# Packing normed attention outputs into dense rows for the output projection, and moving weight loads to SyncE

## The chip, the cores and the metric

The kernel runs on one core of a Trainium2 chip. The metric is the device time of one execution in microseconds. Before the change it is 2338.6 us, the median of three runs (2338.2 to 2338.93). The profiled execution spans 2337.2 us.

A core has five engines with an instruction stream each. TensorE (PE) multiplies matrices; its loads of the stationary operand are listed as PEld. VectorE (DVE) and ScalarE (ACT) work element by element, GpSimd (POOL) does the same and issues transfers, and SyncE (SP) only issues transfers. Each engine takes its instructions in order, and waits on semaphores for what others produce.

## The reference

Four attention layers on x of shape 1 x 2048 x 640, with 32 heads of 20 columns. Layers 0 and 2 (kind A) look back over a window of 256 positions; layers 1 and 3 (kind B) are full, with no mask.

```python
def ref(x, wqkv, wo, windowed):
    q, k, v = split(x @ wqkv)                      # 32 heads of 20 columns
    scores = einsum("bhqd,bhkd->bhqk", q, k) * 20 ** -0.5
    if windowed:
        scores = where((i - j >= 0) & (i - j < 256), scores, -1e9)
    p = softmax(scores)
    o = einsum("bhqk,bhkd->bhqd", p, v)
    return o.transpose(0, 2, 1, 3).reshape(B, S, D) @ wo

x = A_x                                            # A_x: 1 x 2048 x 640, bf16
x = x + ref(layernorm(x), A_wqkv, A_wo, True)
x = x + ref(layernorm(x), B_wqkv, B_wo, False)
x = x + ref(layernorm(x), A_wqkv, A_wo, True)
x = x + ref(layernorm(x), B_wqkv, B_wo, False)
```

## The kernel before

The positions are cut into 4 chunks of 512 (NC = 4, C = 512) and the heads into 8 groups of 4 (G = 8). A unit is one chunk of queries with one head group. Its scores, three banks of 512 columns at a time, go from TensorE to PSUM; ScalarE takes the exponential of all three banks with one instruction; TensorE multiplies the result with the values. One such round is a tick. Everything else is written as generators that a small scheduler at build time interleaves between the scores and the values of a tick: normalisation, the q, k and v projections, the tails of units, the output projections. Each gives up its turn with `yield`: `("wait", n)` sleeps n ticks, `("hold", cost)` keeps an accumulation together, `("pe", cost)` charges TensorE time. Layer l + 1 starts on a chunk before layer l has finished the others, so a windowed unit stands between full ones.

In a head group, head j of the group has the 20 rows from 32j, and its 12 other rows carry nothing for the output. The output weights are loaded in the same form, 8 tiles of 128 rows of which 80 count:

```python
    def load_wop(w):
        v = wo_in[w].rearrange("(g j e) f -> j e g f", g=G, j=4)
        for j in range(4):
            nc.sync.dma_start(out=wop[32 * j : 32 * j + DH, :, :], in_=v[j])
```

The tail of a unit divides by the sums of the softmax and leaves the normed output of head group g in `on[:, g, :]`:

```python
    def t_tail(l, c, g, on, oT):
        # ... row sums, reciprocal, transpose, spread over rows into PSUM bank zb, with waits of 2 ticks ...
        nc.vector.tensor_tensor(out=on[:, g, :], in0=oT[:], in1=zb, op=ALU.mult)     # L1043
        drop_m(mb)
        yield ("pe", 0.3)
        fill(3)
        ready.add(("tail", l, c, g))
        if (l, c, g) == (3, NC - 1, G - 3):
            push("before_last", t_before_last(), 0, 8.0)
        if g == G - 1:
            # ... push t_out(l, c) and, below layer 3, the work of layer l + 1 on this chunk ...
```

The output projection of a chunk multiplies and adds the residual, in 8 accumulations of 8 matmuls. The very last chunk is split: `t_before_last` does head groups 0 to 5 early, `t_out` only the last two.

```python
    def t_out(l, c):
        # ...
        for qb in range(4):
            for i in range(2):
                mb = yield from take_m()
                yp = ps[:, mb, 0:HD]
                g0 = G - 2 if last else 0
                for g in range(g0, G):
                    nc.tensor.matmul(                                                # L532
                        yp, lhsT=on[:, g, qb * P : (qb + 1) * P],
                        rhs=wop[:, g, i * HD : (i + 1) * HD],
                        start=(g == g0), stop=(g == G - 1),
                    )
                    if g < G - 1:
                        yield ("hold", 0.14)
                # ... x_sb = x_sb + yp on VectorE (L541) ...
        # ...
        n = out_n[0] = out_n[0] + 1
        if n < len(out_seq) and out_seq[n] != out_seq[n - 1]:
            load_wop(out_seq[n])
```

The q and k projections take their weights in 160 KB blocks of 128 columns. A block is asked for some ticks ahead, and from then on the projection waits at least 4 ticks before it is built in:

```python
    def get_w(l, n, c, i):
        t = wqkp.tile([P, KD, P], BF16, name="wqk", tag="wqk")
        wtick[l, n, c, i] = state["tick"] + 4
        if l or c:
            a = n * D + i * P
            nc.gpsimd.dma_start(out=t[:], in_=wq_view[l % 2][:, :, a : a + P])       # L318
            return t
        # ... the first chunk of layer 0 is cut out of a larger load ...
```

The normalisation transposes each tile of 128 positions, and in layers 0 and 1 puts two matmuls ahead of it whose result nobody reads. They keep TensorE busy. The program also counts activity and adds such matmuls in `keep_clock` where the count is low:

```python
            mb = yield from take_m()                                                 # in t_ln
            for _ in range(2*(l<2)):
                unread(mb)
            # ... 5 transposes of 128 columns into ps[:, mb] ...

    def unread(b):
        nc.tensor.matmul(                                                            # L611
            ps[:, b, :], lhsT=ident[:], rhs=masks[:, 0, :], start=True, stop=True
        )
        state["heat"] += 1.0

                warmth = 1.76 if state["unit"] >= woven else 1.0                     # in the main loop
                state["least"] = warmth * n_b / 3 if state["unit"] < index[3, 1, 0, None] else 0.0
                load_ahead()
                r = rate(t)
                pump(r, r + 0.1)          # advance waiting tasks by r
                keep_clock()
```

SyncE issues all loads of queries, keys and values of the units (`load_unit`: nine for a full unit, eight for a windowed one), the output weights and the final stores. GpSimd issues the weight blocks and the stores of q, k and v to DRAM.

Of the kernel before, what the change touches and what calls it, by code (L numbers as in the profile page):

```python
# [12 lines left out]
ALU = mybir.AluOpType  # L13
ACT = mybir.ActivationFunctionType

P = 128
# [3 lines left out]
DH = 20  # L20
NT = S // P
KD = D // P
G = 8
C = 512
NC = S // C
EPS = 1e-5
SCALE = DH ** -0.5
HD = D // 2
# [21 lines left out]
def kernel(  # L50
# [10 lines left out]
    nc = tc.nc  # L61
# [27 lines left out]
    wo_in = (A_wo, B_wo)  # L89
# [5 lines left out]
    wop = big.tile([P, G, D], BF16, name="wop", tag="wop")  # L95
# [13 lines left out]
    op = ps[:, 7, :]  # L109
# [6 lines left out]
    wq_view = [w.rearrange("(c p) f -> p c f", p=P) for w in wqkv_in]  # L116
# [3 lines left out]
    for h in range(2):  # L120
        for n in range(2):
            a = n * D + h * HD
# [3 lines left out]
        nc.sync.dma_start(out=x_sb[:, 4 * c : 4 * c + 4, :], in_=xin[:, 4 * c : 4 * c + 4, :])  # L126
    nc.sync.dma_start(out=wv_sb[1][:], in_=wq_view[1][:, :, 2 * D : 3 * D])

    def load_wop(w):
        v = wo_in[w].rearrange("(g j e) f -> j e g f", g=G, j=4)  # L130
        for j in range(4):
            nc.sync.dma_start(out=wop[32 * j : 32 * j + DH, :, :], in_=v[j])
# [3 lines left out]
        out=ident[:], in_=ident[:], compare_op=ALU.not_equal, fill=1.0,  # L136
# [6 lines left out]
    for m, b, ge in (  # L143
# [4 lines left out]
        v = masks[:, m, b * P : (b + 1) * P]  # L148
        nc.gpsimd.affine_select(
            out=v, in_=v, compare_op=ALU.is_ge if ge else ALU.is_gt, fill=0.0,  # L150
# [161 lines left out]
    def get_w(l, n, c, i):  # L312

        t = wqkp.tile([P, KD, P], BF16, name="wqk", tag="wqk")
        wtick[l, n, c, i] = state["tick"] + 4
        if l or c:
            a = n * D + i * P
            nc.gpsimd.dma_start(out=t[:], in_=wq_view[l % 2][:, :, a : a + P])  # L318
            return t
        tv = t[:].rearrange("p c (j m) -> p c j m", j=4)  # L320
        nc.gpsimd.memset(tv[:, :, :, DH:32], 0.0)
        src = raw[:, :, n * D + 80 * i : n * D + 80 * (i + 1)]
        nc.vector.tensor_copy(
            out=tv[:, :, :, 0:DH], in_=src.rearrange("p c (j e) -> p c j e", j=4)
        )
        wtick[l, n, c, i] = 0
        return t
# [48 lines left out]
    def t_ln(l, c):  # L376
        while ("x", l, c) not in ready:
            yield ("wait", 1)
        yield from room("xnT", "ln")
        for n in (1, 0):  # L380
            order = worder[l, n]
            if order and not any(e in wtiles for e in order):
                wtiles[order[0]] = get_w(*order[0])
        users[l, c] = 9 if (l, c) == (0, 0) else (11, 12, 11, 11)[l]
        mv = mvs.pop((l, c))
        rstd = lnp.tile([P, 4], F32, name="rstd", tag="rstd")
        nc.gpsimd.tensor_scalar(  # L387
            out=rstd[:], in0=mv[:, :, 1], scalar1=EPS, scalar2=1.0, op0=ALU.add, op1=ALU.mult
        )
        nc.gpsimd.tensor_tensor(out=rstd[:], in0=rstd[:], in1=nhalf[:], op=ALU.pow)  # L390
        yield ("wait", 2)
        nmr = lnp.tile([P, 4], F32, name="nmr", tag="nmr")
        nc.vector.scalar_tensor_tensor(
            out=nmr[:], in0=mv[:, :, 0], scalar=-1.0, in1=rstd[:], op0=ALU.mult, op1=ALU.mult
        )
        xt = xtp.tile([P, KD, C], BF16, name="xnT", tag="xnT")
        for i in range(4):
            xn = xnp.tile([P, D], BF16, name="xn", tag="xn")
            nc.vector.tensor_scalar(
                out=xn[:], in0=x_sb[:, 4 * c + i, :],  # L400
                scalar1=rstd[:, i : i + 1], scalar2=nmr[:, i : i + 1],
                op0=ALU.mult, op1=ALU.add,
            )
            yield ("wait", 1)
            mb = yield from take_m()
            for _ in range(2*(l<2)):
                unread(mb)
            trp = ps[:, mb, :].bitcast(BF16)[:, 0 : KD * P].rearrange("p (c m) -> p c m", c=KD)
            for dc in range(KD):
                nc.tensor.transpose(  # L410
                    out=trp[:, dc, :], in_=xn[:, dc * P : (dc + 1) * P], identity=ident[:]
                )
            evac(xt[:, :, i * P : (i + 1) * P], trp)
            drop_m(mb)
            yield ("pe", 0.4)
        xnT[l, c] = xt
        live["ln"] -= 1
        ready.add(("xnT", l, c))
# [98 lines left out]
    out_seq = [0] * 4 + [1, 0] * 4 + [1] * 4  # L517
    out_n = [0]

    def t_out(l, c):  # L520
        on = ons[l, c]
        last = (l, c) == (3, NC - 1)
        while last and "before_last" not in ready:
            yield ("wait", 1)
        assert out_seq[out_n[0]] == l % 2
        for qb in range(4):
            for i in range(2):
                mb = yield from take_m()
                yp = ps[:, mb, 0:HD]
                g0 = G - 2 if last else 0  # L530
                for g in range(g0, G):
                    nc.tensor.matmul(  # L532
                        yp, lhsT=on[:, g, qb * P : (qb + 1) * P],
                        rhs=wop[:, g, i * HD : (i + 1) * HD],
                        start=(g == g0), stop=(g == G - 1),
                    )
                    if g < G - 1:
                        yield ("hold", 0.14)
                xv = x_sb[:, 4 * c + qb, i * HD : (i + 1) * HD]
                had = part_o["t"][:, 2 * qb + i, 0:HD] if last else xv  # L540
                nc.vector.tensor_tensor(out=xv, in0=had, in1=yp, op=ALU.add)  # L541
                drop_m(mb)
                yield ("pe", 0.14)
            if l < 3:
                stats(l + 1, c, qb)
            else:
                nc.sync.dma_start(out=xout[:, 4 * c + qb, :], in_=x_sb[:, 4 * c + qb, :])
        ons.pop((l, c))
        ready.add(("out", l, c))
        ready.add(("x", l + 1, c))  # L550
        n = out_n[0] = out_n[0] + 1
        if n < len(out_seq) and out_seq[n] != out_seq[n - 1]:
            load_wop(out_seq[n])

    def t_before_last():

        on = ons[3, NC - 1]
        for qb in range(4):
            for i in range(2):
                mb = yield from take_m()  # L560
                yp = ps[:, mb, 0:HD]
                for g in range(G - 2):
                    nc.tensor.matmul(
                        yp, lhsT=on[:, g, qb * P : (qb + 1) * P],
                        rhs=wop[:, g, i * HD : (i + 1) * HD],
                        start=(g == 0), stop=(g == G - 3),
                    )
                    if g < G - 3:
                        yield ("hold", 0.14)
                xv = x_sb[:, 4 * (NC - 1) + qb, i * HD : (i + 1) * HD]  # L570
                nc.vector.tensor_tensor(
                    out=part_o["t"][:, 2 * qb + i, 0:HD], in0=xv, in1=yp, op=ALU.add
                )
                drop_m(mb)
                yield ("pe", 0.14)
        ready.add("before_last")
# [32 lines left out]
# [6 lines that stand above are left out]
# [382 lines left out]
    def t_tail(l, c, g, on, oT):  # L997
        def fill(count):

            for n in range(count * ((l, c, g) == (3, NC - 1, G - 1))):  # L1000
                nc.tensor.matmul(
                    ps[:, 0, :], lhsT=ident[:], rhs=masks[:, 0, :], start=True, stop=True
                )
# [3 lines left out]
        mb = yield from take_m()  # L1007
        warm_bank(mb)
        zp = ps[:, mb, 0:16]
        for qb in range(4):  # L1010
            nc.tensor.matmul(
                zp[:, 4 * qb : 4 * qb + 4], lhsT=oT[:, qb * P : (qb + 1) * P],
                rhs=sel4[:], start=True, stop=True,
# [11 lines left out]
        mb = yield from take_m()  # L1025
# [9 lines left out]
        mb = yield from take_m()  # L1035
        warm_bank(mb)
        zb = ps[:, mb, :]
        for qb in range(4):
            nc.tensor.matmul(  # L1039
                zb[:, qb * P : (qb + 1) * P], lhsT=spread4[:, qb, :], rhs=rT[:],  # L1040
                start=True, stop=True,
            )
        nc.vector.tensor_tensor(out=on[:, g, :], in0=oT[:], in1=zb, op=ALU.mult)  # L1043
        drop_m(mb)
        yield ("pe", 0.3)
        fill(3)
        ready.add(("tail", l, c, g))
        if (l, c, g) == (3, NC - 1, G - 3):
            push("before_last", t_before_last(), 0, 8.0)
# [5 lines left out]
    def t_zeros():  # L1055

        z = ka_all[:, G : G + 4, :].rearrange("p a b -> p (a b)")
        yield ("wait", 4)
        for n in range(2):
            nc.gpsimd.dma_start(  # L1060
                out=wop[:, 4 * n : 4 * n + 3, :].rearrange("p g f -> p (g f)"), in_=z[:, 0 : 3 * D]
            )
            nc.gpsimd.dma_start(out=wop[:, 4 * n + 3, :], in_=z[:, 0:D])
            yield ("wait", 1)
        load_wop(0)
        for t in (*kts, *qts):
            nc.gpsimd.dma_start(out=t[:], in_=z[:, 0 : t.shape[1]])
            yield ("wait", 1)
        ready.add("kts")
# [67 lines left out]
    with tc.manual_schedule():  # L1137
# [14 lines left out]
        n = 0  # L1152
# [54 lines left out]
        t = -1  # L1207
        ended = None
        closed = -2
        while ended is None or t < ended + 8:  # L1210
# [3 lines left out]
            if t < len(tiles) or banks:  # L1214
# [54 lines left out]
                i = 0  # L1269
# [115 lines left out]
```

## Time and profile before

| Stretch, us | ScalarE busy | TensorE busy | TensorE clock |
|---|---|---|---|
| 0 to 350 | 288.1 of 350.0 | 315.2 | 0.99 |
| 350 to 700 | 327.7 of 350.0 | 302.7 | 0.96 |
| 700 to 1165 | 441.2 of 465.0 | 395.8 | 0.96 |
| 1165 to 1640 | 455.7 of 475.0 | 401.7 | 0.99 |
| 1640 to 2337 | 666.8 of 697.2 | 577.3 | 0.57 |

The last stretch is layer 3 alone, with no q, k or v projection left. The clock is the share of full speed that TensorE was granted. The difference between length and busy time of ScalarE is its idle time, 157.7 us over the whole span.

The chain of work that ended last, by engine:

```
ACT 40%; PE 27%; issue 17%; DVE 13%; DMA 1%; POOL 1%; ACTq 0%; SPq 0%; DVEq 0%; POOLq 0%; another core or an unknown queue 0%
```

Two of the groups of transfers (how many, KB each, median us from issue to landing where the profile has it):

```
wqk<-in_B_wqkv_dram POOLq DMA_DIRECT2D x80, 160.0 KB, 3.8
wqk<-in_A_wqkv_dram POOLq DMA_DIRECT2D x70, 160.0 KB, 3.3
```

In a line of a group, the name of the code line comes first, then engine and operation, what is written from what is read, shape and count; after the bar the busy time in us and the mean of one in ns; after the second bar how long the engine sat idle just before these instructions, and what ended most of that. Matmuls overlap, so the mean of one is its latency and not its spacing. In a timeline, the first two columns are start and length in us, and the bracket at the end is the idle time before and what ended it.

### The profile page before, as it was taken

The page shows a single profiled execution, that of the slowest core. Times are in us where ns is not written, and L with a number is a line of the kernel's source. Part 1 is how long each engine was busy: PE and PEld are TensorE (multiplying, and loading weights), DVE is VectorE, ACT ScalarE, POOL GpSimd, SP SyncE. Part 2 cuts the span into 40 slices and gives each one's busy share as a digit, 9 for nine tenths or more (in the row PEclk, how much of TensorE's full clock was granted, in tenths as well). Part 3 has the DMA queues.
Part 4 walks back from the last instruction along what each step waited for, and adds up shares of the span by engine and source line. Part 5 has one row for each costly group of instructions (what it writes and reads, how often), then busy time and mean ns, then how long its engine had stood idle before and what let it go on. Part 6 is the DMA issues. An engine that isn't in the chain of part 4 may idle for free.

```text
span 2337.2 us, 40427 instructions
## 1 busy us (share of the span) xinstructions
PE 1992.5 (85%) x15613; PEld 722.9 (31%) x15773; DVE 1464.3 (63%) x2724; ACT 2179.5 (93%) x1753; POOL 271.1 (12%) x445
## 2 busy tenths in 40 slices
PE   8899988888888888888888898888888888888887
PEld 3444333333223332323323333333322222222222
DVE  6677775426646666656667644452577777777772
ACT  7788989899999988999899999999999999999997
POOL 3332311200200112001120013001000000000000
PEclk9999999999989999999999999999855565556556
DMA  5232321321300223102231023112210010011100
GB/s 183 81 103 80 107 65 56 90 68 48 89 21 25 58 68 90 43 14 58 70 99 31 17 82 107 41 28 76 65 30 27 26 38 27 27 35 39 31 14 12
DMA packets 84881, 132.57 MB, mean 57 GB/s; under 512 B 19760, under 2 KB 60080, under 8 KB 84688
## 3 DMA queue, kind: packets, MB, share of 16 engines
q1 hardware_dynamic: 65472, 76.80, 11.9%
q0 software_dynamic: 19216, 53.17, 7.8%
q8 instruction: 124, 2.03, 0.4%
q14 instruction: 69, 0.57, 0.1%
HBM read 98.70 MB, written 27.79 MB: 54 GB/s over the span
## 4 chain that ended last, share of the span: by engine, by line
ACT 40%; PE 27%; issue 17%; DVE 13%; DMA 1%; POOL 1%; ACTq 0%; SPq 0%; DVEq 0%; POOLq 0%; another core or an unknown queue 0%
ACT pt L1275 39%; PE ps L1244 7%; PE ps L353 5%; PE ps L532 4%; PE ps L1308 4%; DVE pt L1344 3%; PE ps L446 2%; PE ps L611 2%; DVE on L1043 1%; DVE st L304 1%; DMA wqk<-in_B_wqkv_dram 1%; ACT ka L1275 1%; DVE oT L830 1%; DVE raw_o L878 1%; PE ps L410 1%
## 5 line engine op out<-in xcount | busy, mean ns | idle before, releaser
L1275 ACT ACTIVATE pt<-ps 128x1536 bf16<-128x1536 f32 (+2 forms) x1641 | 2100.9, 1492 | 115.2 <-PE ps L1244 104.6
L1244 PE MATMUL ps<-qt,kt 32*128 32x512 bf16 x4008 | 644.6, 457 | 197.1 <-ACT pt L1275 164.2
L1308 PE MATMUL ps<-pt,vt 128*21 128x512 bf16 x3860 | 469.2, 458 | 5.1 <-issue 2.2
L1244 PEld LDWEIGHTS <-kt 32*128 32x128 bf16 x4008 | 191.0, 93 | 615.1 <-issue 592.0
L1344 DVE TENSOR_TENSOR pt<-pt,masks 128x1024 bf16<-128x1024 bf16 (+5 forms) x403 | 239.0, 626 | 131.5 <-ACT pt L1275 131.0
L611 PE MATMUL ps<-masks,ident 128*128 128x512 bf16 x672 | 231.7, 393 | 27.0 <-DVE rT L1030 9.6
L353 PE MATMUL ps<-xnT,wqk 128*128 128x512 bf16 x767 | 211.4, 388 | 24.8 <-DMA wqk<-in_B_wqkv_dram 4.2
L1308 PEld LDWEIGHTS <-vt 128*21 128x21 bf16 x3960 | 100.0, 90 | 319.1 <-issue 309.7
L304 DVE CAST st<-ps 128x512 bf16<-128x512 f32 x127 | 87.8, 691 | 154.4 <-PE ps L353 150.8
L532 PE MATMUL ps<-wop,on 128*128 128x320 bf16 x976 | 165.5, 312 | 6.9 <-DVE x_sb L541 2.5
L1244 PE MATMUL ps<-qa,ka 32*128 32x384 bf16 (+2 forms) x1408 | 116.8, 275 | 33.9 <-ACT pt L1275 28.8
L878 DVE TENSOR_SCALAR xnT<-ps 128x512 int32<-128x512 f32 x88 | 60.8, 691 | 106.3 <-PE ps L871 105.9
L1043 DVE TENSOR_TENSOR on<-oT,ps 128x512 bf16<-128x512 bf16 x128 | 87.5, 683 | 59.5 <-PE ps L1039 59.2
L830 DVE CAST oT<-ps 128x512 bf16<-128x512 f32 x112 | 76.9, 686 | 70.8 <-PE ps L1308 45.4
L446 PE MATMUL ps<-wv,xnT 128*128 128x320 bf16 x640 | 111.9, 309 | 7.0 <-DVE va L304 1.6
L541 DVE TENSOR_TENSOR x_sb<-x_sb,ps 128x320 bf16<-128x320 bf16 x120 | 57.9, 482 | 95.1 <-PE ps L532 94.9
L532 PEld LDWEIGHTS <-on 128*128 128x128 bf16 x976 | 90.2, 101 | 71.4 <-issue 38.4
L353 PEld LDWEIGHTS <-wqk 128*128 128x128 bf16 x830 | 71.3, 98 | 114.0 <-issue 49.2
L387 POOL TENSOR_SCALAR rstd<-mv 128x4 f32<-128x4 f32 x15 | 4.0, 265 | 815.6 <-DVE mv L374 815.5
L611 PEld LDWEIGHTS <-ident 128*128 128x128 bf16 x768 | 56.4, 97 | 126.2 <-issue 123.0
L1308 PE MATMUL ps<-pt,va 128*21 128x384 bf16 (+2 forms) x1408 | 77.6, 281 | 4.9 <-DVE pt L1344 2.9
L1244 PEld LDWEIGHTS <-ka 32*128 32x128 bf16 x1408 | 44.4, 92 | 101.2 <-issue 92.7
(107 smaller groups left out, 1790.9 us busy)
## 6 DMA issues: line engine op xcount, KB each, us to landing
vt<-v_d SPq DMA_DIRECT2D x48, 336.0 KB
kt<-k_d SPq DMA_DIRECT2D x192, 80.0 KB
wqk<-in_B_wqkv_dram POOLq DMA_DIRECT2D x80, 160.0 KB, 3.8
wqk<-in_A_wqkv_dram POOLq DMA_DIRECT2D x70, 160.0 KB, 3.3
k_d<-st POOLq DMA_DIRECT2D x75, 128.0 KB, 2.1
q_d<-st POOLq DMA_DIRECT2D x75, 128.0 KB, 2.1
qt<-q_d SPq DMA_DIRECT2D x384, 20.0 KB
v_d<-vs POOLq DMA_DIRECT2D x16, 336.0 KB, 3.1
```

The lines of the kernel that those rows point to most:

```text
L304: nc.vector.tensor_copy(out=out_, in_=in_)
L353: nc.tensor.matmul(pq, lhsT=wt[:, dc, :], rhs=xt[:, dc, :], start=(dc == 0), stop=(dc == KD - 1),)
L446: nc.tensor.matmul(pv, lhsT=xt[:, dc, i * P : (i + 1) * P], rhs=wv_sb[l % 2][:, dc, h * HD : (h + 1) * HD], start=(dc == 0), stop=(dc == K ...
L532: nc.tensor.matmul(yp, lhsT=on[:, g, qb * P : (qb + 1) * P], rhs=wop[:, g, i * HD : (i + 1) * HD], start=(g == g0), stop=(g == G - 1),)
L611: nc.tensor.matmul(ps[:, b, :], lhsT=ident[:], rhs=masks[:, 0, :], start=True, stop=True)
L830: nc.vector.tensor_copy(out=oT[:], in_=op)
L878: V.tensor_scalar(out=xi.bitcast(I32)[:, i * C : (i + 1) * C], in0=side["psum"], scalar1=SCALE * LOG2E * E23, scalar2=127.0 * E23, op0=ALU ...
L1043: nc.vector.tensor_tensor(out=on[:, g, :], in0=oT[:], in1=zb, op=ALU.mult)
L1244: nc.tensor.matmul(sp[:, i, col * P : (col + qn) * P], lhsT=u.k(kc, j), rhs=u.q(j, q0, qn), start=True, stop=True,)
L1275: nc.scalar.activation(out=pt[:, i:k, b0 * P :], in_=sp[:, i:k, b0 * P :], func=ACT.Exp, scale=SCALE,)
L1308: nc.tensor.matmul(op[32 * j : 32 * j + VW, q0 * P : (q0 + qn) * P], lhsT=u.v(kc, j), rhs=pg[:, i, col * P : (col + qn) * P], start=(first ...
L1344: nc.vector.tensor_tensor(out=pt_[:, i:k, b0 * P :], in0=pt_[:, i:k, b0 * P :], in1=mv_, op=ALU.mult,)
```

## The change

From layer 1 on, the normed output of a head group goes to one of three spare slots of `on` (5 to 7), and two ticks later SyncE is given transfers from SBUF to SBUF that copy the 20 rows of each head to their place in 640 dense rows, five blocks of 128. The output weights are loaded in the same dense form. The projection then takes 5 matmuls in an accumulation instead of 8. The last two head groups of the last chunk keep the old form, so that no transfer stands at the very end; the first part of that chunk takes 4 matmuls instead of 6. Layer 0 keeps the old form.

Two further things change. Weight blocks are loaded by SyncE instead of GpSimd. And the two unread matmuls ahead of the transposes are gone.

```diff
+    def packed(l, c):
+        return l > 0
+
-    def load_wop(w):
+    def load_wop(w, dense):
+        if dense:
+            nc.sync.dma_start(out=wop[:, 0:KD, :], in_=wo_in[w].rearrange("(b p) f -> p b f", p=P))
+            if w and out_n[0] == 4:
+                ...                      # once: groups 6 and 7 in the old form, for the last chunk
+            return
@@ get_w
-            nc.gpsimd.dma_start(out=t[:], in_=wq_view[l % 2][:, :, a : a + P])
+            nc.sync.dma_start(out=t[:], in_=wq_view[l % 2][:, :, a : a + P])
@@ t_ln
             mb = yield from take_m()
-            for _ in range(2*(l<2)):
-                unread(mb)
@@ t_out
+        dense = packed(l, c) and not last
+        a, b = (0, KD) if dense else (G - 2 if last else 0, G)
-                for g in range(g0, G):
+                for g in range(a, b):
@@ t_before_last
-                for g in range(G - 2):
+                for b in range(4):
+                    n = min(P, (G - 2) * 80 - b * P)
                     nc.tensor.matmul(
-                        yp, lhsT=on[:, g, qb * P : (qb + 1) * P],
+                        yp, lhsT=on[0:n, b, qb * P : (qb + 1) * P],
@@ t_tail
-        nc.vector.tensor_tensor(out=on[:, g, :], in0=oT[:], in1=zb, op=ALU.mult)
+        end = (l, c) == (3, NC - 1) and g >= G - 2
+        spread = packed(l, c) and not end
+        nu = on[:, 5 + g % 3 if spread else g, :]
+        nc.vector.tensor_tensor(out=nu, in0=oT[:], in1=zb, op=ALU.mult)
         drop_m(mb)
         yield ("pe", 0.3)
         fill(3)
+        if spread:
+            yield ("wait", 2)
+            for j in range(4):
+                r, a = (4 * g + j) * DH, 0
+                while a < DH:
+                    b, o = divmod(r + a, P)
+                    n = min(DH - a, P - o)
+                    nc.sync.dma_start(
+                        out=on[o : o + n, b, :], in_=nu[32 * j + a : 32 * j + a + n, :]
+                    )
+                    a += n
         ready.add(("tail", l, c, g))
```

More of the change, by code (lines that the diff above doesn't have):

```diff
@@ L127 @@
     nc.sync.dma_start(out=wv_sb[1][:], in_=wq_view[1][:, :, 2 * D : 3 * D])
-    def load_wop(w):
+    def packed(l, c):
[4 more added lines that the diff above has]
+            if w and out_n[0] == 4:
+                v = wo_in[w].rearrange("(g j e) f -> j e g f", g=G, j=4)
+                for j in range(4):
+                    nc.sync.dma_start(
+                        out=wop[32 * j : 32 * j + DH, G - 2 : G, :], in_=v[j][:, G - 2 : G, :]
+                    )
+            return
         v = wo_in[w].rearrange("(g j e) f -> j e g f", g=G, j=4)
@@ L529, in t_out @@
                 yp = ps[:, mb, 0:HD]
-                g0 = G - 2 if last else 0
-                for g in range(g0, G):
+                for g in range(a, b):
                     nc.tensor.matmul(
@@ L534, in t_out @@
                         rhs=wop[:, g, i * HD : (i + 1) * HD],
-                        start=(g == g0), stop=(g == G - 1),
+                        start=(g == a), stop=(g == b - 1),
                     )
-                    if g < G - 1:
+                    if g < b - 1:
                         yield ("hold", 0.14)
@@ L551, in t_out @@
         n = out_n[0] = out_n[0] + 1
-        if n < len(out_seq) and out_seq[n] != out_seq[n - 1]:
-            load_wop(out_seq[n])
+        if n < len(out_seq) and (n == 4 or out_seq[n] != out_seq[n - 1]):
+            load_wop(out_seq[n], n >= 4)
     def t_before_last():
@@ L561, in t_before_last @@
                 yp = ps[:, mb, 0:HD]
-                for g in range(G - 2):
+                for b in range(4):
+                    n = min(P, (G - 2) * 80 - b * P)
                     nc.tensor.matmul(
-                        yp, lhsT=on[:, g, qb * P : (qb + 1) * P],
-                        rhs=wop[:, g, i * HD : (i + 1) * HD],
-                        start=(g == 0), stop=(g == G - 3),
+                        yp, lhsT=on[0:n, b, qb * P : (qb + 1) * P],
+                        rhs=wop[0:n, b, i * HD : (i + 1) * HD],
+                        start=(b == 0), stop=(b == 3),
                     )
-                    if g < G - 3:
+                    if b < 3:
                         yield ("hold", 0.14)
@@ L1046, in t_tail @@
         fill(3)
+        if spread:
+            yield ("wait", 2)
+            for j in range(4):
+                r, a = (4 * g + j) * DH, 0
+                while a < DH:
+                    b, o = divmod(r + a, P)
+                    n = min(DH - a, P - o)
+                    nc.sync.dma_start(
+                        out=on[o : o + n, b, :], in_=nu[32 * j + a : 32 * j + a + n, :]
+                    )
+                    a += n
         ready.add(("tail", l, c, g))
@@ L1064, in t_zeros @@
             yield ("wait", 1)
-        load_wop(0)
+        load_wop(0, False)
         for t in (*kts, *qts):
```

## The prediction

> **What bounds the kernel now.** I read the busy shares first, then the 40 slices, then the costliest groups, then a table of stretches, and last the timeline of single stretches. The busy shares and the slices:
>
> ```profile
> PE 1992.5 (85%) x15613; PEld 722.9 (31%) x15773; DVE 1464.3 (63%) x2724; ACT 2179.5 (93%) x1753; POOL 271.1 (12%) x445
> ...
> ACT  7788989899999988999899999999999999999997
> ...
> PEclk9999999999989999999999999999855565556556
> ```
>
> ScalarE computes the exponentials for 2179.5 of 2337.2 us. Nothing in the change removes an exponential, so 2337.2 - 2179.5 = 157.7 us of ScalarE idle time is all that there is to win, and the question is which part of it the change touches. The groups:
>
> ```profile
> L1275 ACT ACTIVATE pt<-ps 128x1536 bf16<-128x1536 f32 (+2 forms) x1641 | 2100.9, 1492 | 115.2 <-PE ps L1244 104.6
> ...
> L611 PE MATMUL ps<-masks,ident 128*128 128x512 bf16 x672 | 231.7, 393 | 27.0 <-DVE rT L1030 9.6
> L353 PE MATMUL ps<-xnT,wqk 128*128 128x512 bf16 x767 | 211.4, 388 | 24.8 <-DMA wqk<-in_B_wqkv_dram 4.2
> ...
> L532 PE MATMUL ps<-wop,on 128*128 128x320 bf16 x976 | 165.5, 312 | 6.9 <-DVE x_sb L541 2.5
> ```
>
> Of the 115.2 us in which L1275 sat idle, 104.6 ended when the scores (L1244) came from TensorE. TensorE serves scores, values, projections and warming matmuls in one order, so ScalarE starves where a burst of other matmuls stands between two sets of scores. The stretches of the last layer show it cleanly (columns: length, then busy time of PE, PEld, DVE, ACT, POOL):
>
> ```profile
> 1752.90:1869.80 116.90, 97.03 (x601) 24.10 (x600) 92.34 (x134) 116.90 (x87) 0.00 (x0) 0.50 0.09 27
> 1869.76:1986.60 116.84, 97.40 (x634) 28.23 (x631) 88.79 (x130) 112.18 (x83) 0.00 (x0) 0.59 0.11 32
> ```
>
> The first has no output projection and ScalarE is never idle. The second has one group of 64 output matmuls and ScalarE loses 116.84 - 112.18 = 4.7 us. The timeline of an earlier such group shows how:
>
> ```profile
> 1669.26 2.31 PE L532 MATMUL ps<-wop,on 128*128 128x320 bf16 x8
> 1671.50 0.10 PEld L1308 LDWEIGHTS <-vt 128*21 128x21 bf16 x4 [0.52 <-issue]
> 1671.50 0.61 PE L1308 MATMUL ps<-pt,vt 128*21 128x512 bf16 x4
> ...
> 1672.04 0.61 PE L1244 MATMUL ps<-qt,kt 32*128 32x512 bf16 x3
> ...
> 1672.76 1.45 ACT L1275 ACTIVATE pt<-ps 128x1536 bf16<-128x1536 f32 x1 [1.41 <-PE ps L1244]
> ...
> 1679.53 1.26 PE L532 MATMUL ps<-wop,on 128*128 128x320 bf16 x8
> ```
>
> Eight matmuls take 2.31 us at the half clock in which this layer runs, later scores are late by as much, and ScalarE waits 1.41 us. Once the clock is up, eight take 1.26 us and the gaps shrink to 0.19-0.39 us.
>
> **What the Trainium skill says.** (1) "TensorE: Matmul & The Clock Gate", section "Wait — 56ns, not 53.3ns?": back-to-back matmuls start N columns at 2.4 GHz plus about 2.5 ns apart when warm, N at 1.2 GHz when cold; contraction rows don't enter. For 320 columns that is 136 and 267 ns. The trace agrees: eight in 1.26 us with 0.30 us for one alone is (1.26 - 0.30)/7 = 137 ns; cold, (2.31 - 0.474)/7 = 262 ns. So filling 128 rows instead of 80 costs a matmul nothing and 5 for 8 is a true saving. (2) The same page, section "What's actually happening": the clock has two states, and activity releases the throttle. The trace agrees, with a clock of 0.50 in the stretch without projections and 0.59 in the one with them. Fewer matmuls may delay the rise. (3) "DMA: Bandwidth & Descriptors", section "Anatomy of one DMA — SWDGE (gpsimd) path": about 2 us fixed for one transfer, and waits are served on the issuing sequencer before dispatch, so a queue is blocked behind a waiting entry. The trace shows 2.1 us from issue to landing for the 128 KB key stores. It shows no SBUF-to-SBUF transfer, so my 2 us for one is an estimate from these stores.
>
> **Part A, the output projection.** From layer 1 on there are 12 groups (3 layers of 4 chunks); 11 drop 3 of 8 matmuls in each of 8 accumulations, 264, and the first part of the last group drops 2 of 6 in each of 8, 16. Together 280.
> - Layer 3, three groups. Cold, a burst shrinks by 3 x 0.262 = 0.79 us, so a 1.41 us gap becomes about 0.6 and the 0.81 us gap after it about 0. Warm, it shrinks by 3 x 0.137 = 0.41 us, as large as the largest gap of 0.39. So of about 4.7 us a group some 1.3 stays: 3.4 x 3 = 10 us won. The split last group has gaps of 1.48 and 1.18 us in the timeline at 2277 and 2280, about 3 us in all, and drops 2 of 6: 1.5 us won. Together 11.5.
> - Layers 1 and 2, eight groups: 8 x 24 x 0.137 = 26 us of TensorE. But ScalarE's gaps that lie beside an output burst, added up in the timeline from 700 to 1640 us, are only 7.4 us; I take 5 of them as won. The rest of the 26 us is TensorE time that was not on the path, and part will be refilled: the program adds warming matmuls (L611) whenever its count of activity falls below 1.76 per three banks, and an output burst now adds 3.2 to that count instead of 5.1.
> - Cost: the packing. Every chunk needs 32 heads plus 4 heads split at a 128-row border, 36 transfers; 11 x 36 + 27 = 423 transfers of about 20 KB. SyncE issues one every 0.375 us (seven issues from 1057.09 to 1059.35 us, six steps of 0.377). That is 159 us of SyncE over 1700 us, on a queue that now issues some 1,150, or 430 us. The last four of a chunk all land in the fifth block. They can go once VectorE has the normed output, land after about 4 x 0.375 + 2 = 3.5 us (estimate), and the projection may follow two ticks (2.7 us, at 1.36 us a tile) plus four matmuls later. I count 0.5 us of TensorE stall in each of the eight mid groups and 1 us in each of four in layer 3, which has less slack: 4 + 4 = 8 us lost, the least certain figure here.
> Net of A: 11.5 + 5 - 8 = 8.5 us won.
>
> **Part B, two warming matmuls fewer per normalised tile.** Layers 0 and 1 have 3 + 4 such chunks of 4 tiles, 2 each: 56 matmuls. L353, also of 512 columns, runs five in 1.25 us with 0.376 for one, 0.22 us apart; 56 x 0.22 = 12 us of TensorE. 24 fall in the first 350 us, where ScalarE is idle for 62 us and TensorE is most crowded; half of their 5 us should show, 2.5. Of the 7 us in layer 1 the program gives most back as other warming matmuls; 1.5 show. Won: 4 us.
>
> **Part C, weights by SyncE.** TensorE waited for weight blocks for this long:
>
> ```profile
>   DMA wqk<-in_B_wqkv_dram: 10.5, 12
> ```
>
> (from the waits of L353's two instruction kinds.) At 446.17 us, for example, GpSimd issued a weight load only after it had stood behind a value store, and TensorE then waited until 449.96, ScalarE for 1.36 us. SyncE has no such store ahead of it, and I count 6 of the 10.5 us as won. But its own bursts take its place: a full unit's 9 loads and a small unit's 8 are 17 x 0.375 = 6.4 us, as long as the four ticks that the program leaves a weight load. I count 3 us lost. Net: 3 us won. The 132 us of GpSimd time that the 150 weight issues took is on no path by itself.
>
> Sum: 8.5 + 4 + 3 = 15.5 us, to which I add 2 for projections that start earlier because the same share of TensorE time now moves more work. 2338.6 - 17.5 = 2321 us.
>
> **Rivals.** First, the transfers replace the wait: if each of the 11 groups stalls TensorE for 3 us rather than 0.5 to 1, ScalarE loses some 25 us more and the time is about 2345. For it: the new issues stand in the same queue as value and key loads and the 800 KB output weights; against it: the data leave VectorE two ticks earlier and SyncE is idle four fifths of the time. Second, SyncE's order hurts the weights: its longest waits are for buffers and stores,
>
> ```profile
> SPq L744 <- PE ps L1317: 577.2, 25, 37.7
> ...
> SPq L736 <- DMA q_d<-st: 146.3, 20, 36.2
> ```
>
> and a weight load behind one of these is late. Against it: L744's 577 us are in layer 3, where no weights are loaded, and SyncE waits there because nothing else was due. With 75 weight loads in the first 600 us, 10 late by 2 us would give 2338. Third, the clock: without the warming matmuls the array may fall to half speed around the normalisations of layers 0 and 1 (clock 0.93 from 584 to 701 us already); one such fall for 5 us costs about 2.5, seven would cost 17, and the time would be about 2336. Fourth, the good case: all of layer 3's gaps and all weight stalls vanish and the landings are hidden, some 30 us, 2308.
>
> **Range and chances.** Three of the rivals add 15 to 25 us, and I give each one chance in five or six; the good case takes 13 off. That makes 2303 to 2344 for eight in ten. Two per cent is 47 us: below 2292 would need nearly a third of ScalarE's idle time, and above 2385 would need 4 us lost at every group. 0.04, 0.93, 0.03.
>
> **What would show it.** Right: ScalarE's busy time stays within 5 us of 2179; the output matmuls fall from 976 to about 712; the stretches of layer 3 with a projection show ScalarE idle for 1 to 2.5 us instead of 4.7; the waits of L353 for weights halve. Wrong: output matmuls waiting more than 2 us a group for a transfer into the packed rows, or weight waits above 10.5 us, or a TensorE clock below 0.93 before 700 us. The estimate itself fails most easily in the landing stall and in how the program's own scheduling reacts to the two ticks and the changed activity count.

## The result, and the profile after

The changed kernel takes 2369.6 us (median of four runs, 2362.5 to 2376.5) beside 2338.8 us for the kernel before on the same chip: 1.28 per cent slower, with an interval of 0.94 to 1.61. The prediction was 2321 us. The profiled execution spans 2360.8 us, 23.6 more than before.

Busy engines and the groups that answer to those shown of before, from the page of the changed kernel (columns as explained above; line numbers have moved: L1302 is the exponentials, L366 the q and k projections, L544 the output projection):

```profile
PE 1982.1 (84%) x15306; PEld 695.7 (29%) x15465; DVE 1458.2 (62%) x2724; ACT 2178.7 (92%) x1753; POOL 144.0 (6%) x295
...
L1302 ACT ACTIVATE pt<-ps 128x1536 bf16<-128x1536 f32 (+2 forms) x1641 | 2101.3, 1499 | 138.4 <-PE ps L1271 128.5
...
L366 PE MATMUL ps<-xnT,wqk 128*128 128x512 bf16 x758 | 216.2, 394 | 31.3 <-DMA wqk<-in_B_wqkv_dram 6.1
...
L544 PE MATMUL ps<-wop,on 128*128 128x320 bf16 x712 | 135.3, 324 | 27.3 <-DMA on<-on 17.6
```

ScalarE does the same work, 2178.7 us against 2179.5, and the output matmuls fell from 976 to 712 and from 165.5 to 135.3 us, as foretold. But ScalarE sat idle before L1302 for 138.4 us instead of 115.2, and the output matmuls for 27.3 instead of 6.9. Their waits have a new name: transfers into the packed rows.

One group in layer 3, from the timeline of the changed kernel:

```profile
1918.70 0.58 PE L1052 MATMUL ps<-rT,spread 32*128 32x128 bf16 x4
...
1919.71 0.68 DVE L1059 TENSOR_TENSOR on<-oT,ps 128x512 bf16<-128x512 bf16 x1
1920.41 3.02 SPq L1070 DMA_DIRECT2D on<-on  x4
...
1921.27 1.25 PE L544 MATMUL ps<-wop,on 128*128 128x320 bf16 x4
...
1924.66 0.45 PE L544 MATMUL ps<-wop,on 128*128 128x320 bf16 x1 [2.15 <-DMA on<-on]
...
1926.30 1.45 ACT L1302 ACTIVATE pt<-ps 128x1536 bf16<-128x1536 f32 x1 [2.94 <-PE ps L1271]
```

VectorE has the normed output at 1920.39. SyncE needs 3.02 us to issue four transfers, 0.75 us each. TensorE starts the projection at 1921.27, does four matmuls, and stands for 2.15 us before the fifth, which reads the rows just sent. ScalarE loses 2.94 us. Read in this way from the timeline, the stalls of the twelve groups add up to 21.1 us; one group has none.

### The profile page after: what moved, and what is told of

It reads as the page before. It is cut to its first block, busy times and chain, and to the rows that moved or that the text cites. A ratio compares the mean times of both kernels' runs of the same rounds, so it can differ in the third digit from the quotient of the medians.

```text
span 2360.8 us, 40369 instructions
## 1 busy us (share of the span) xinstructions
PE 1982.1 (84%) x15306; PEld 695.7 (29%) x15465; DVE 1458.2 (62%) x2724; ACT 2178.7 (92%) x1753; POOL 144.0 (6%) x295
## 5 line engine op out<-in xcount | busy, mean ns | idle before, releaser
L1302 ACT ACTIVATE pt<-ps 128x1536 bf16<-128x1536 f32 (+2 forms) x1641 | 2101.3, 1499 | 138.4 <-PE ps L1271 128.5
L1271 PE MATMUL ps<-qt,kt 32*128 32x512 bf16 x4008 | 651.9, 463 | 190.7 <-ACT pt L1302 159.1
L1335 PE MATMUL ps<-pt,vt 128*21 128x512 bf16 x3860 | 475.4, 464 | 5.7 <-issue 1.6
L624 PE MATMUL ps<-masks,ident 128*128 128x512 bf16 x654 | 224.4, 389 | 28.0 <-DVE rT L1043 9.4
L366 PE MATMUL ps<-xnT,wqk 128*128 128x512 bf16 x758 | 216.2, 394 | 31.3 <-DMA wqk<-in_B_wqkv_dram 6.1
L544 PE MATMUL ps<-wop,on 128*128 128x320 bf16 x712 | 135.3, 324 | 27.3 <-DMA on<-on 17.6
L457 PE MATMUL ps<-wv,xnT 128*128 128x320 bf16 x640 | 117.5, 316 | 5.2 <-DVE vs L317 1.1
L366 PEld LDWEIGHTS <-wqk 128*128 128x128 bf16 x830 | 71.1, 99 | 126.0 <-issue 54.3
L544 PEld LDWEIGHTS <-on 128*128 128x128 bf16 x712 | 64.4, 103 | 88.6 <-issue 53.9
L1271 PEld LDWEIGHTS <-ka 32*128 32x128 bf16 x1408 | 45.1, 92 | 102.7 <-issue 94.5
L457 PEld LDWEIGHTS <-xnT 128*128 128x128 bf16 x640 | 56.3, 101 | 53.0 <-issue 34.0
```

The source lines that it names most:

```text
L366: nc.tensor.matmul(pq, lhsT=wt[:, dc, :], rhs=xt[:, dc, :], start=(dc == 0), stop=(dc == KD - 1),)
L457: nc.tensor.matmul(pv, lhsT=xt[:, dc, i * P : (i + 1) * P], rhs=wv_sb[l % 2][:, dc, h * HD : (h + 1) * HD], start=(dc == 0), stop=(dc == K ...
L544: nc.tensor.matmul(yp, lhsT=on[:, g, qb * P : (qb + 1) * P], rhs=wop[:, g, i * HD : (i + 1) * HD], start=(g == a), stop=(g == b - 1),)
L624: nc.tensor.matmul(ps[:, b, :], lhsT=ident[:], rhs=masks[:, 0, :], start=True, stop=True)
L1271: nc.tensor.matmul(sp[:, i, col * P : (col + qn) * P], lhsT=u.k(kc, j), rhs=u.q(j, q0, qn), start=True, stop=True,)
L1302: nc.scalar.activation(out=pt[:, i:k, b0 * P :], in_=sp[:, i:k, b0 * P :], func=ACT.Exp, scale=SCALE,)
```

## The experiments

The change has three parts: P, the packed rows; W, the weights on SyncE; U, the unread matmuls taken out. The landing theory says that P's transfers stall the projection; the queue theory, that W's blocks come late on SyncE; the clock theory, that U lets TensorE's clock fall. All ratios are to the kernel before on the same chip, with 95 per cent intervals. Where us are given for a ratio, they are the ratio's distance from 1 times 2342 us, the median of before beside these runs.

| Kernel | Parts | Ratio | Interval | us against before |
|---|---|---|---|---|
| u_only | U | 1.0014 | 1.0001 to 1.0028 | +3 |
| w_only | W | 1.0019 | 1.0000 to 1.0038 | +4 |
| p_only | P | 1.0096 | 1.0061 to 1.0131 | +22 |
| pu | P, U | 1.0109 | 1.0078 to 1.0140 | +26 |
| wu | W, U | 1.0060 | 1.0022 to 1.0097 | +14 |
| five_only | short sums, no packing | 0.9944 | 0.9926 to 0.9962 | -13 |
| p_wait | P, projection 4 ticks later | 0.9969 | 0.9954 to 0.9984 | -7 |
| p_six | P without groups 6 and 7 | 0.9975 | 0.9964 to 0.9986 | -6 |
| p_six_wait | the same, one wait more | 0.9969 | 0.9955 to 0.9983 | -7 |
| p_two | P, last transfers on two queues | 0.9992 | 0.9970 to 1.0013 | -2 |
| w_lead | W, weights 8 ticks ahead | 1.0020 | 1.0002 to 1.0039 | +5 |
| b_lead | before, weights 8 ticks ahead | 1.0059 | 1.0039 to 1.0079 | +14 |
| pu_wait | P, U, 4 ticks later | 1.0009 | 0.9989 to 1.0029 | +2 |
| pw_wait | P, W, 4 ticks later | 1.0112 | 1.0042 to 1.0182 | +26 |
| after_wait | P, W, U, 4 ticks later | 1.0077 | 1.0046 to 1.0107 | +18 |

**One part at a time.** w_only and u_only change one place in before; p_only is the changed kernel with both put back; pu puts back the weights alone.

```diff
 w_only
-            nc.gpsimd.dma_start(out=t[:], in_=wq_view[l % 2][:, :, a : a + P])
+            nc.sync.dma_start(out=t[:], in_=wq_view[l % 2][:, :, a : a + P])
 u_only
-            for _ in range(2*(l<2)):
-                unread(mb)
```

> The kernel before with one line changed: the 150 weight blocks are issued by SyncE. The order of instructions on TensorE is that of before. Queue theory (weight blocks stand behind the unit loads on SyncE): 10 to 18 us slower, TensorE waits of L353 for weights rise from 10.5 to over 20 us, and runs spread by more than before's 0.2 per cent. Landing theory (the changed kernel lost its time to the transfers into the packed rows alone) and clock theory: within 3 us of before.

> The kernel before without the two unread matmuls ahead of the transposes; nothing else differs. Clock theory: slower by 5 to 15 us, with a TensorE clock below 0.97 between 117 and 350 us. Landing and queue theory: 2 to 6 us faster, as part B of the prediction had it, 4.

> The kernel before with the packed rows and 5 matmuls alone; weights by GpSimd and the unread matmuls as before. Landing theory: 5 to 15 us slower, because each group stalls TensorE for some 2 to 3 us at its fifth matmul (about 30 us of waits for transfers into the packed rows), more than the 8.5 us that the shorter bursts win net in the prediction. Queue or clock theory: 5 to 12 us faster, as the prediction's part A had it.

> The changed kernel with weights issued by GpSimd again: packed rows and no unread matmuls. If the three parts add up, it is p_only plus what u_only differs from before, within 4 us. Queue theory: 10 to 18 us faster than the changed kernel's 2370 us. Landing theory: within 4 us of the changed kernel.

P alone costs 22 us, W and U 4 and 3, each at the edge of what can be told from nothing. Unrounded the three add up to 1.29 per cent or 30 us, and the changed kernel stands 1.28 per cent above before. So most of the loss is P's, as the landing theory has it, though 22 us is more than the 5 to 15 that it said; p_only's stalls at the first wait of each group add up to 25.4 us in its timeline, in 11 of 12 groups. pu is p_only plus u_only within 1 us, and misses what the queue theory said of it (10 to 18 us under the changed kernel): it is within 5. w_only's 4 us meet neither the queue theory's 10 to 18 nor the 3 of the others. u_only lies at +3, against the 4 us gain expected; its clock is 0.95 in both of the first two stretches, where before had 0.99 and 0.96, so it went the clock theory's way, by less than that theory said. The stretch from 117 to 350 us, before and then in u_only (columns as in the table of stretches of the prediction, with clock, DMA share and GB/s at the end):

```profile
117.00:350.00 233.00, 215.37 (x2041) 93.14 (x2065) 175.91 (x387) 201.74 (x187) 69.15 (x106) 0.99 0.31 89
```

```profile
117.00:350.00 233.00, 213.67 (x1988) 90.83 (x1988) 170.94 (x378) 195.92 (x182) 68.44 (x105) 0.95 0.30 86
```

ScalarE is idle for 37.1 us there instead of 31.3. The traces of all six kernels without the unread matmuls have a clock of 0.93 to 0.95 in this stretch, and those of all others 0.96 to 0.99.

w_only's runs go from 2327.6 to 2367.5 us, and its ratio leaves out the four slowest of twenty as runs in a slower state. With them its median is 5.6 us above before, so W may cost somewhat more than 4. Its profile is that of the slowest run, so no size is taken from it here, only what its clock did.

**What five for eight is worth, and what the stall costs.** five_only multiplies head groups 0 to 4 of 8 only, from layer 1 on, and leaves the others out of its output; there is no packing in it. p_wait is p_only with the projection held back:

```diff
 five_only
+                g1 = G if last or l == 0 else KD
-                for g in range(g0, G):
+                for g in range(g0, g1):
 p_wait
+        if spread and (g == G - 1 or (l, c, g) == (3, NC - 1, G - 3)):
+            yield ("wait", 4)
         ready.add(("tail", l, c, g))
```

p_six leaves head groups 6 and 7 in the old form, so that six matmuls are needed and the transfers are a whole head group older when a projection starts.

> The kernel before with the short accumulations and no packing at all: from layer 1 on the projection multiplies only head groups 0 to 4 of 8 (0 to 3 of 6 in the first part of the last group), the other groups are left out of its output. It measures what 5 matmuls for 8 are worth without any transfer. The prediction's part A put that at 16.5 us (11.5 in layer 3, 5 in layers 1 and 2): expected 12 to 20 us faster than before. Rival (the burst was not what held ScalarE up, or fewer matmuls cost the clock): within 5 us of before.

> p_only with four more ticks (some 5.4 us) between the last head group's transfers and the moment at which the output projection may start; nothing else differs. Landing theory: the stalls at the fifth matmul (25 us in p_only) shrink to under 4 us, the time falls by 20 to 30 us from p_only and lands near five_only, 8 to 18 us below before. Rival (the cost is SyncE's time, or the load on the DMA engines from the 423 transfers, which stay): within 6 us of p_only.

> p_only with head groups 6 and 7 left in the old form in every chunk, so that six matmuls are needed instead of five and no transfer stands just ahead of a projection; 27 transfers a chunk instead of 36. Landing theory: no stall on transfers; it keeps two thirds of what five matmuls win, so 6 to 12 us faster than before. Rival (SyncE's time or DMA load): three quarters of p_only's loss remain, so some 10 us slower than before.

five_only is 13 us faster than before. The prediction's 16.5 us for the shorter bursts was close. p_wait has all 423 transfers and no work taken away; it is 29 us faster than p_only and 7 us faster than before, one short of the 8 to 18 expected. So neither SyncE's time nor the load on the DMA engines was the main cost: the moment was. The group of the output projection in p_wait:

```profile
L546 PE MATMUL ps<-wop,on 128*128 128x320 bf16 x712 | 126.9, 312 | 9.2 <-DVE x_sb L555 5.0 <-DVE rz L1031 1.6 <-DVE on L1061 1.5
```

No transfer is left among its waits, and the idle time is 9.2 us. In the timelines, ScalarE's gaps that lie beside an output burst add up, from 480 us on, to 24.0 us before, 10.6 in five_only, 46.4 in p_only and 13.1 in p_wait. Against before that is 13 us less in five_only and 22 more in p_only, about what the times of these two differ by; p_wait, with 11 less, is 7 faster. p_six, with six matmuls, gets 6 us. Between five_only and p_wait lie 6 us, which the transfers or the later start of the projection may cost; the two intervals overlap, and where these us are lost stays open.

**Which term of the stall.** p_two sends the last four transfers by two queues:

```diff
+                    two = g == G - 1 or (l, c, g) == (3, NC - 1, G - 3)
+                    q = nc.gpsimd if two and j >= 2 else nc.sync
-                    nc.sync.dma_start(
+                    q.dma_start(
```

> p_only with the last four transfers ahead of a projection shared out, two issued by SyncE and two by GpSimd, at the same tick. If the stall at the fifth matmul is the time to issue four transfers one after the other (0.75 us each), it falls from 2.3 us by about 1.5 us a group, and the time by 10 to 18 us from p_only. If it is the fixed time from the last issue to landing, or GpSimd's own issue is as slow, the stall stays within 0.5 us of 2.3 and the time within 5 us of p_only.

> p_six, with four more ticks ahead of the first part of the last group's projection alone, the only place where p_six still waited for a transfer (2.6 us). Landing theory: 1 to 3 us faster than p_six, so 7 to 9 us faster than before. Rival (that stall is hidden in the last layer): as p_six.

In p_two the stalls are 0 to 1.13 us, 7.3 us over the twelve groups instead of 25.4, 1.5 us less in the mean. That is two issues of 0.75 us. The group that answers to the one shown of the changed kernel:

```profile
1896.65 1.52 SPq L1074 DMA_DIRECT2D on<-on  x2
...
1897.51 1.25 PE L546 MATMUL ps<-wop,on 128*128 128x320 bf16 x4
1899.49 0.43 PE L546 MATMUL ps<-wop,on 128*128 128x320 bf16 x1 [0.73 <-DMA on<-on]
```

GpSimd issues its two beside these in 1.01 us, and 1.3 us after SyncE's last issue TensorE goes on. The time falls by 24 us from p_only, more than the stalls did and more than the 10 to 18 expected. So the issue of four transfers one after the other makes up most of the stall: with two of them taken off the queue, 7.3 of 25.4 us are left. p_six_wait differs from p_six by less than the intervals can tell; its median is 1 us lower, and its rival, that the one stall of p_six hid, isn't ruled out.

**The weights on SyncE.** w_lead is w_only, and b_lead is before, with `state["tick"] + 8` for `+ 4`.

> w_only with at least eight ticks instead of four between the request for a weight block and its projection. Queue theory (a weight block is late because it stands behind up to 17 unit loads on SyncE): the waits of L353 for weights fall from over 12 us to under 5 us, and the time is 3 to 8 us below w_only unless the later projections crowd elsewhere. Rival (the many 256-byte pieces of a weight block slow other transfers): waits for unit loads stay, and so does the time.

> The kernel before, weights by GpSimd, with at least eight ticks instead of four between the request for a weight block and its projection. It is the control of w_lead, whose waits for weights were gone and whose time was still 0.2 per cent above before. If the longer lead costs something by itself (projections are crowded later): 3 to 8 us slower than before, and w_lead's queue waits were the cost of w_only after all. If the lead is free or helps (0 to 5 us faster), then moving the weights to SyncE costs some 5 us in another way than by late blocks.

w_lead's waits for weights are gone, but its time is that of w_only: the queue theory's number failed. b_lead, the control, gives a reason: the longer lead by itself costs 14 us, where 3 to 8 were expected. With the same lead of eight ticks, SyncE stands 0.4 per cent below GpSimd (1.0020 beside 1.0059; the intervals meet at 1.0039, and each ratio is to before on its own chip); with four it does not. That points to weights on SyncE costing only where they come late, without proving it. That they come late, undisturbed by packing, can be read from wu beside u_only, which differ in W alone. The line of wu, then that of u_only, from their waits (total us, times, longest):

```profile
PE ps L353 <- DMA wqk<-in_B_wqkv_dram: 8.7, 6, 2.9
```

```profile
PE ps L353 <- DMA wqk<-in_B_wqkv_dram: 3.7, 5, 1.6
```

**Does the stall's cure mend the changed kernel?** after_wait is the changed kernel with p_wait's two lines.

> The changed kernel with four more ticks between the last head group's transfers and the output projection. If the parts add up: p_wait's 7 us under before plus u_only's 3 and w_only's 4, so within 5 us of before and 25 to 30 us faster than the changed kernel. If the weights on SyncE and the transfers hinder each other on the same queue: 5 to 15 us slower than before.

It is 12 us faster than the changed kernel stood, but 18 us above before, where the sum of parts would be about 0 and two users hindering each other were given 5 to 15. Three more kernels leave one part out each: U back (pw_wait), weights back (pu_wait), no packing (wu).

> after_wait with the weights issued by GpSimd: packed rows with the later projection, no unread matmuls. If the excess of after_wait needs the weights on SyncE: p_wait's -7 plus u_only's +3, so 0 to 8 us below before. If packing and the missing unread matmuls hinder each other: 10 or more above before.

> after_wait with the unread matmuls back: packed rows with the later projection, weights on SyncE. If the two users of SyncE's queue hinder each other: 10 us or more above before, waits of L366 for weights well above w_only's. If the excess needs the missing unread matmuls (late weights and a falling clock together): -7 plus 4, so 0 to 6 us below before.

> The kernel before with weights on SyncE and without the unread matmuls, no packing. If late weights and the missing matmuls reinforce each other through the clock: 15 us or more above before, with a clock under 0.93 between 117 and 467 us. If they only add: 5 to 10 us above before.

pu_wait is at +2, above the 0 to 8 us below before that were expected, but far from after_wait. wu is at +14 where W and U add up to 7; its interval, 5 to 23 us, leaves open whether they only add, and its clock between 117 and 467 us is 0.94, not under 0.93. pw_wait is at +26, with four runs from 2346.9 to 2379.8 us. So the excess is largest where P and W stand together, two users of one queue. From the timeline of pw_wait, of its run of 2378.7 us:

```profile
633.84 4.44 SPq L1072 DMA_DIRECT2D on<-on  x5
...
638.32 0.49 SPq L751 DMA_DIRECT2D qa<-q_d  x1
...
641.53 0.97 SPq L331 DMA_DIRECT2D wqk<-in_A_wqkv_dram  x2
...
644.32 0.61 PE L366 MATMUL ps<-xnT,wqk 128*128 128x512 bf16 x1 [5.33 <-DMA wqk<-in_A_wqkv_dram]
...
646.12 1.45 ACT L1306 ACTIVATE pt<-ps 128x1536 bf16<-128x1536 f32 x1 [4.89 <-PE ps L1275]
```

Five packing transfers hold SyncE for 4.44 us, eight unit loads for 3.2 us more, and only then are the weights issued; TensorE waits 5.33 us and ScalarE 4.89. TensorE's waits of this kind in pw_wait, and after them the one in p_wait:

```profile
PE ps L366 <- DMA wqk<-in_A_wqkv_dram: 16.2, 7, 5.3
...
PE ps L366 <- DMA wqk<-in_B_wqkv_dram: 8.2, 6, 2.9
```

```profile
PE ps L366 <- DMA wqk<-in_B_wqkv_dram: 4.8, 6, 1.6
```

24.4 us against 4.8. From 518 us on, where the packing begins, these waits are 14.4 us in pw_wait (the first line) and 0.3 in wu (the second), which has the same queue without packing; p_wait, with packing and the weights on GpSimd, has none:

```profile
PE ps L366 <- DMA wqk<-in_A_wqkv_dram: 14.4, 6, 5.3
```

```profile
PE ps L353 <- DMA wqk<-in_A_wqkv_dram: 0.3, 1, 0.3
```

So these waits need both users. But not all of pw_wait's excess is this. Its first packing transfer is issued at 518 us, and before that, from 350 to 450 us, it has already lost 16 us of ScalarE to p_wait (columns as in the table of stretches of the prediction; pw_wait first):

```profile
350.00:400.00 50.00, 45.71 (x329) 13.53 (x326) 25.73 (x52) 40.56 (x35) 4.54 (x8) 0.72 0.24 61
400.00:450.00 50.00, 47.90 (x282) 13.65 (x286) 17.32 (x37) 36.66 (x31) 0.00 (x0) 0.59 0.07 17
```

```profile
350.00:400.00 50.00, 45.38 (x411) 16.05 (x409) 28.24 (x59) 47.72 (x44) 9.28 (x13) 1.00 0.23 65
400.00:450.00 50.00, 46.58 (x368) 18.99 (x367) 23.62 (x52) 45.87 (x41) 5.88 (x10) 1.00 0.24 68
```

The clock is 0.72 and 0.59 where p_wait has 1.00. after_wait has such a dip in the same place (0.74, 0.82), and so has the profile of w_only (0.81, 0.75), without any packing; w_lead, wu and the changed kernel, with weights on SyncE too, do not. It seems to come in some executions of kernels with W. No wait of TensorE for weights lies between 284 and 465 us in pw_wait's trace, so a late block just ahead of the dip is not its cause; what sets it off was not tested. It stays open too why W costs 4 us beside p_only's stalls (pu to the changed kernel) and 16 once they are cured (pu_wait to after_wait). Part of it is that TensorE's waits for weights from 490 us on are 4.3 us in the changed kernel and 11.2 in after_wait.

## Why the prediction was wrong

**The bound and the bursts: right.** ScalarE's busy time stayed within 1 us, and 5 matmuls for 8 win 13 us where part A had 16.5. By stage, ScalarE's gaps beside output bursts fell in five_only from 7.4 to 2.3 us between 700 and 1640 us (5 won, as foretold, though all of ScalarE's idle time in this stretch went from 43.1 to 45.1), and in layer 3 from 16.3 to 8.3 (8 won instead of 11.5).

**The landing stall: the term that was mis-sized, and it turned the sign.** Part A counted "0.5 us of TensorE stall in each of the eight mid groups and 1 us in each of four in layer 3", 8 us. p_only shows 25.4. The groups ahead of layer 3 were given the larger slack, and they lost most: ScalarE's gaps beside output bursts between 700 and 1640 us are 26.4 us in p_only against 7.4 before, and in layer 3 15.7 against 16.3, where the shorter bursts won as much as the stalls cost. Two steps failed. The first is "SyncE issues one every 0.375 us", read from loads out of DRAM and applied to transfers inside SBUF; these take 0.75 us each, twice that, for the same 20 KB. The second is the head start: "the projection may follow two ticks (2.7 us, at 1.36 us a tile) plus four matmuls later", counted from VectorE's result. The ticks run from TensorE's spread matmuls. In the group shown these start at 1918.70, the projection at 1921.27, 2.57 us later; but VectorE's result comes at 1920.39, so of the two ticks only 0.88 us are left; in the eleven groups of p_only that stall it is 0.8 to 1.4 us. Data at 1920.4 plus 3.0 us of issue plus about 1.2 us to landing meets a fifth matmul that was ready at 1922.5. So the head start was 1.8 us short, while issue and landing together took 4.2 us for the 3.5 estimated: the head start was the larger of the two errors. The first rival had this mechanism and said 3 us a group and 2345 us. Its stalls were nearly right and its time was not: ScalarE loses more than TensorE does (2.94 us for 2.15 in the group shown), and the rival still counted 9 us as won by parts B and C and by earlier projections, where B and C cost 7.

**Part B: wrong in sign.** The unread matmuls were to give 4 us and their removal costs 3. The third rival named the clock; it is lower with U, and of the 56 matmuls removed the program's own count put back only 2 (15,773 weight loads, one for each matmul, before; 15,719 in u_only), so "the program gives most back" failed.

**Part C: wrong in sign, and one reading was wrong.** The line under "TensorE waited for weight blocks for this long", with its 10.5 us, adds the same waits twice: 6.3 us of LDWEIGHTS and 4.2 of matmuls that stood behind them. So there was less to win than the 6 us counted. The cost, SyncE's bursts, was named and put at 3 us; W alone costs 4 net. In the changed kernel the waits for these blocks, counted in the same double way, are 13.6 us, above the mark of 10.5 that the prediction had set for being wrong. What was not foreseen is that the packing's transfers would stand ahead of the weights, since the two were summed as if they had separate queues. Two counts of the prediction are off without bearing on its sum: SyncE issues 774 transfers in the last 1700 us of before, not 1,150, and the first 600 us hold 77 weight loads, not 75.

**The range** let each rival come alone, on top of gains that were taken as sure. P by itself, at 22 us above before, was already beyond the high end of 2344, and 4 from the queue and 3 from the clock came with it. One sign of being right failed too: in the stretch of layer 3 from 1869.76 to 1986.60 us, ScalarE is idle for 4.0 us in the changed kernel, against 4.7 before and the 1 to 2.5 named.

## What to carry to other kernels

A transfer between a producer and its consumer is timed from the producer's end to the consumer's arrival, with the issue time of that very kind of transfer times their number; if it lands late, start the consumer later or share the last issues over two queues before giving the idea up: four ticks turned 22 us lost into 7 won. Don't put what TensorE will wait for on a queue that has just been given another burst: the costs of two users of one queue didn't add here (24.4 us of waits for weights in pw_wait, against 9.0 in wu and 4.8 in p_wait). When a wait is summed over instruction kinds, ask first whether one kind stood behind the other.

## What the runs showed that was not expected

- A transfer of 20 KB from SBUF to SBUF takes SyncE a median 0.71 us to issue, against 0.28 to 0.33 us for one of 20 KB from DRAM.
- The same 150 weight blocks are cut into far more packets on SyncE's queue:

```profile
DMA packets 185416, 140.47 MB, mean 60 GB/s; under 512 B 119814, under 2 KB 167814, under 8 KB 185222
```

  That is the changed kernel; before had 84,881 packets, 19,760 of them under 512 bytes, and w_lead, with the same transfers as before and weights on SyncE, has 173,680 and 115,760. The blocks' rows are 256 bytes long. w_lead is not slower than b_lead, so no cost of this by itself shows.
- A clock of 0.59 held over 50 us in which TensorE's instructions covered 47.9 us (pw_wait), so a TensorE that is busy by the profile can stay at the low clock.
